# Float64 weights converted in pieces of 768 columns, with the lower parts on DVE and no arithmetic on GpSimd meanwhile

## The chip, the cores and the metric

The kernel runs as one program on one core of a Trainium2 chip. The metric is the device time of one execution in microseconds. PE is TensorE, DVE is VectorE, ACT is ScalarE, POOL is GpSimd and SP is SyncE, whose queue issues the loads.

## The reference

Three blocks follow one another. The gated layer's three weight matrices reach the kernel as float64, in pairs of 32-bit words; all else is float32.

```python
# sliding-window attention: B, H, S, D = 4, 8, 576, 64, window 64
scores = where(0 <= i - j < 64, q @ k.T / 8, -1e9)
x = softmax(scores) @ v                       # -> 2304 tokens x 512
# gated layer: w_gate, w_val 512 x 1536, w_out 1536 x 512
x = (sigmoid(x @ w_gate) * (x @ w_val)) @ w_out
# 8 experts, top 1: w1 512 x 1024, w2 1024 x 512 each
e = argmax(x @ w_gate2);  y = relu(x @ w1[e]) @ w2[e]
out = softmax(x @ w_gate2)[e] * sigmoid(x @ w_output_gate)[e] * y
```

## The kernel before

Attention is cut into 36 blocks of 64 queries, each with four pairs of heads. A block has four stages: `st_s` makes scores on PE, row maxima on DVE and exponentials with their sums on ACT; `st_n` takes the reciprocal of the sums on DVE and multiplies the probabilities by it (line 217), for the first `PM_B` = 12 blocks on POOL, for the rest on DVE; `st_t` transposes on PE and copies on ACT; `st_v` multiplies with the values and splits the result into an upper part `xh` (ACT) and a lower part `xl` (DVE). Four blocks make a chunk of 256 tokens; there are nine chunks c.

The gated layer walks over steps (c, f), f being one of 12 slices of 128 hidden columns. `g1(c, f)` runs 24 matmuls (line 300), three for each product, since every operand is split into an upper and a lower part. Then come a tanh on ACT (303), a product on DVE (304), the upper part `gh` on ACT (307) and the lower part `gl` on POOL (308). `g2` adds the slice to the chunk's sums with six matmuls (319), one step later. The steps of chunks 0 and 1 are interleaved, because the weights are still being converted; there are 24 of these, and chunks 2 to 8 follow with weights that stay in SBUF.

A slice f has 1536 float64 columns per partition: gate, value and output weights of 512 each. They are loaded and converted in 36 pieces of 512. `load_w` loads a piece of 512 KB into one of `B_STG` = 3 staging buffers; pieces 3 to 8 (`RAWS` = 2 slices) go to memory of weight tiles that are filled only later. `conv_a` takes the absolute value of the upper words on ACT (273) into one of `B_Z` = 4 buffers z. `conv_b` runs four instructions on DVE, two with one tensor input (281, 282) and two with two (283, 284), which put the float32 together; ACT copies it rounded as the upper part (286), and POOL subtracts that from z for the lower part (287). A staging buffer is free when line 284 is done, and then SP issues the next load into it.

Order: `FIRST` is the order of the first loads on SP (q: keys and queries of a block, v: values, w: a piece of weights, m and c: tables). `conv` is called after each step and keeps the converted pieces two slices ahead of the steps (`CVX` = 6 pieces); before the first step it does one piece for each of six rounds (`CV_S`). `AHEAD` = 1 says how many pieces `conv_a` is ahead of `conv_b`. The order in which instructions enter each engine's queue comes from a planner that simulates their times when the program is built; each engine then takes its queue in order.

Of the kernel before, what the change touches and what calls it, by code (L numbers as in the profile page):

```python
# [10 lines left out]
F32 = mybir.dt.float32  # L11
F32R = mybir.dt.float32r
BF16 = mybir.dt.bfloat16
I32 = mybir.dt.int32
U32 = mybir.dt.uint32
ACTF = mybir.ActivationFunctionType
ALU = mybir.AluOpType
# [8 lines left out]
P = 128  # L26
# [5 lines left out]
HP = H // 2  # L32
KD = DM // P
NF1 = F1 // P
LAST = NCH - 1, NF1 - 1
# [6 lines left out]
C2L = 0, 1, 2, 3  # L42
A0D = A1D = 2

CVX, CV_S, AHEAD = 6, 1, 1
B_STG, B_Z = 3, 4


PM_B, EARLY, RAWS = 12, 8, 2

FIRST = "q0 m w0 q1 c q2 v0 w1 q3 v1 v2 w2 v3 q4 w3 q5 w4 v4 q6 w5 v5 q7 w6 v6 v7 w7 w8"
WARM_A = 8
WARM_T = 4, 6, 20

# [37 lines left out]
def kern(ctx, tc, ins, out):  # L92
    nc = tc.nc
# [3 lines left out]
    wp = ctx.enter_context(tc.tile_pool(name="wp", bufs=1))  # L97
# [7 lines left out]
    def w_tile(f, n):  # L105

        if (f, n) not in W:
            W[f, n] = wp.tile([P, 6, 512], F32R if n else F32, tag=f"w{f}", name=f"w{f}")
        return W[f, n]
# [13 lines left out]
    stg = cvx.enter_context(tc.tile_pool(name="stg", bufs=B_STG, side="right"))  # L123
    tmp = cvx.enter_context(tc.tile_pool(name="tmp", bufs=B_Z, side="right"))
# [87 lines left out]
    def st_n(b):  # L212
        sp, sm = att[b]
        rs = smp.tile([P, HP], F32, tag="rs", name="rs")
        nc.vector.tensor_scalar(out=rs, in0=sm, scalar1=1e-9, scalar2=None, op0=ALU.add)
        nc.vector.reciprocal(out=rs, in_=rs)
        (nc.gpsimd if b < PM_B else nc.vector).tensor_tensor(out=sp, in0=sp, in1=rs.rearrange("p (h o) -> p h o", o=1).to_broadcast([P, HP, P]), op=ALU.mult)

    def st_t(b):
        sp, sm = att[b]  # L220
# [25 lines left out]
    wst, raws = {}, {}  # L246
    loaded = [0]

    def staged(n):

        return not B_STG <= n < B_STG + 3 * RAWS

    def load_w(_):
        n = loaded[0]
        if n >= 3 * NF1:
            return
        loaded[0] += 1
        if staged(n):
            t = stg.tile([P, 512, 2], I32, tag="stg", name="stg")
        else:  # L260
            f, i = divmod(n - B_STG, 3)
            if i == 0:
                raws[f] = wp.tile([P, 3, 512, 2], I32, tag=f"w{5 - f}", name=f"raw{f}")
            t = raws[f][:, i]
        nc.sync.dma_start(out=t, in_=w1_d[:, n].bitcast(I32).rearrange("p (n t) -> p n t", t=2))
        wst[n] = t

    def conv_a(n):
        if n >= 3 * NF1:
            return  # L270
        raw = wst[n]
        z = tmp.tile([P, 512], F32, tag="z", name="z")
        nc.scalar.activation(out=z, in_=raw[:, :, 1].bitcast(F32), func=ACTF.Abs)
        wst[n] = (raw, z)

    def conv_b(n):
        f, j = divmod(n, 3)
        raw, z = wst.pop(n)
        lo, hi = raw[:, :, 0], raw[:, :, 1]
        zi, hif = z.bitcast(I32), hi.bitcast(F32)  # L280
        nc.vector.tensor_scalar(out=z, in0=z, scalar1=F64_LEAST, scalar2=F64_MOST, op0=ALU.max, op1=ALU.min)  # L281
        nc.vector.tensor_scalar(out=zi, in0=zi, scalar1=3, scalar2=0x3FFFFFF8, op0=ALU.logical_shift_left, op1=ALU.bitwise_and)  # L282
        nc.vector.scalar_tensor_tensor(out=zi, in0=hi, scalar=-0x40000000, in1=zi, op0=ALU.bitwise_and, op1=ALU.bitwise_or)  # L283
        nc.vector.scalar_tensor_tensor(out=zi, in0=lo, scalar=29, in1=zi, op0=ALU.logical_shift_right, op1=ALU.bitwise_or)  # L284
        w = w_tile(f, 1)
        nc.scalar.activation(out=w[:, j], in_=z, func=ACTF.Copy)  # L286
        nc.gpsimd.tensor_tensor(out=w[:, j + 3], in0=z, in1=w[:, j].bitcast(F32), op=ALU.subtract)  # L287
        if staged(n):
            load_w(n)

    gt = {}

    def g1(c, f):
        xh, xl = xt[c]
        g1p = ps.tile([P, 2, CHT], F32, tag="g1", name="g1", bufs=2)
        for j in range(2):
            n = 0
            for k in range(KD):
                for ws, xs in ((j, xh), (j, xl), (j + 3, xh)):
                    nc.tensor.matmul(out=g1p[:, j], lhsT=W[f, 1][:, ws, k * P:(k + 1) * P], rhs=xs[:, k], start=(n == 0), stop=(n == 3 * KD - 1))  # L300
                    n += 1
        g = gp.tile([P, CHT], F32, tag="g", name="g")
        nc.scalar.activation(out=g, in_=g1p[:, 0], func=ACTF.Tanh, scale=0.5)  # L303
        nc.vector.scalar_tensor_tensor(out=g, in0=g, scalar=1.0, in1=g1p[:, 1], op0=ALU.add, op1=ALU.mult)  # L304
        gh = gp.tile([P, CHT], F32R, tag="gh", name="gh")
        gl = gp.tile([P, CHT], F32R, tag="gl", name="gl")
        nc.scalar.activation(out=gh, in_=g, func=ACTF.Copy)  # L307
        (nc.vector if (c, f) == LAST else nc.gpsimd).tensor_tensor(out=gl, in0=g, in1=gh.bitcast(F32), op=ALU.subtract)  # L308
        gt[c, f] = (gh, gl)

    acc = {}
# [307 lines left out]
    def open_stage():  # L619
        sp2 = ctx.enter_context(tc.tile_pool(name="sp2", bufs=1, side="right"))  # L620
        raw2.extend(sp2.tile([P, 1024], F32, name=f"raw{i}") for i in range(3))
        for i in range(3):
            load2(0, i)
# [297 lines left out]
    steps, n1 = [], 0  # L921
# [27 lines left out]
    for c in range(NCH - 1):  # L949
        n = at[c, NF1 - 1] + 1 if c else at[0, NF1 - 1] + 1  # L950
# [7 lines left out]
    nc.vector.memset(hot, 0.0)  # L958
    warm(ps.tile([P, 512], F32, tag="pv", name="idle"), hot, hot[:, 0:P], WARM_A)
    does = dict(q=load_kq, v=load_v, w=load_w, m=lambda _: nc.sync.dma_start(out=msk, in_=m_d[:, 0:M_MID]), c=lambda _: nc.sync.dma_start(out=cst, in_=c_d))  # L960
    for x in FIRST.split():
        does[x[0]](int(x[1:] or 0))
    cw = [0]

    def conv(n):
        n = min(n, 3 * NF1)
        while cw[0] < n:
            conv_a(cw[0] + AHEAD)
            conv_b(cw[0])
            cw[0] += 1  # L970

    for n in range(AHEAD):
        conv_a(n)
    prev = None
    for n in range(min(todo), len(steps)):
        acts = sorted(todo.get(n, []), key=lambda x: (x[0] in ROUTE, x[1]))
        for k, b in acts:
            if k == "n":
                st_n(b)
        if n >= 0:  # L980
            c, f = steps[n]
            g1(c, f)
        for k, b in acts:
            if k in ROUTE:
                ROUTE[k](b)
            elif k != "n":
                dict(s=st_s, t=st_t, v=st_v)[k](b)
        if prev is not None:
            g2(*prev)
            if prev[1] == NF1 - 1:  # L990
                if not R:
                    cvx.close()
                    open_route()
                r_row(prev[0])
        if n < 0:
            conv(cw[0] + CV_S)
        else:
            prev = (c, f)
            if c <= 1:
                conv(3 * sum(x[0] == 0 for x in steps[:n + 1]) + CVX)  # L1000
        if n == at[NCH - 1, 0]:
            atx.close()
            open_stage()
        if (c, f) >= (NCH - 1, 6) and f < NF1 - 1:
            for g in (2 * (f - 6), 2 * (f - 6) + 1):
                if g < NF2:
                    split2(0, g)
# [4 lines left out]
def layout(q, k, v, moe_w_gate, moe_w_val, moe_w_out, moe2_w_gate, moe2_w_output_gate, moe2_w1, moe2_w2):  # L1012
    flat = lambda a: a.transpose(0, 2, 1, 3).reshape(NT, HP, 2 * D)
    kf, vf, qf = flat(k), flat(v), flat(q)
    win = np.arange(P)[None] + BLK * (np.arange(NBLK)[:, None] - 1)
    win[0, :BLK] = np.arange(BLK)
    for b in range(EARLY, NBLK, KR):
        win[b] = np.roll(win[b], BLK)
    kT = kf.reshape(NBLK, BLK, HP, P).transpose(0, 3, 2, 1)
    vw = vf[win].reshape(NBLK, P, DM)  # L1020
    qT = qf.reshape(NBLK, BLK, HP, P).transpose(0, 3, 2, 1)
    kp = lambda w: w.reshape(KD, P, NF1, P).transpose(1, 2, 0, 3).reshape(P, NF1, 512)
    w1 = np.stack([kp(moe_w_gate), kp(moe_w_val), moe_w_out.reshape(NF1, P, DM).transpose(1, 0, 2)], axis=2)
    w1 = np.ascontiguousarray(w1).view(np.int64).reshape(P, 3 * NF1, 512)
    wr = np.concatenate([moe2_w_gate, moe2_w_output_gate], axis=1).reshape(KD, P, 2 * E).transpose(1, 0, 2)
    a = moe2_w1.reshape(E, KD, P, NF2, P).transpose(0, 2, 3, 1, 4).reshape(E, P, NF2, KD * P)
    b = moe2_w2.reshape(E, NF2, P, DM).transpose(0, 2, 1, 3)
    w2 = np.concatenate([a, b], axis=3)
    c, m = const_tables()
    return dict(k=kT, v=vw, q=qT, w1=w1, wr=wr, w2=w2, c=c, m=m)  # L1030
# [19 lines left out]
```

## Time and profile before

| | |
|---|---|
| median of three runs | 919.5 us (914.69, 924.28, 919.5) |
| profiled execution, own time | 917.5 us |
| its span | 915.7 us |
| mean granted clock of PE | 0.98 |
| busy share of the span: PE / DVE / ACT / POOL | 93 / 53 / 40 / 25% |

The span is the time that the trace covers; the execution's own time is 1.8 us longer. Times in the rows below count from the span's start. The shares are averages over very different stages: the first 150 us (attention and conversion), the gated layer up to some 620 us, and the experts.

### The profile page before, as it was taken

The page shows a single profiled execution, that of the slowest core. Times are in us where ns is not written, and L with a number is a line of the kernel's source. Part 1 is how long each engine was busy: PE and PEld are TensorE (multiplying, and loading weights), DVE is VectorE, ACT ScalarE, POOL GpSimd, SP SyncE. Part 2 cuts the span into 40 slices and gives each one's busy share as a digit, 9 for nine tenths or more (in the row PEclk, how much of TensorE's full clock was granted, in tenths as well). Part 3 has the DMA queues.
Part 4 walks back from the last instruction along what each step waited for, and adds up shares of the span by engine and source line. Part 5 has one row for each costly group of instructions (what it writes and reads, how often), then busy time and mean ns, then how long its engine had stood idle before and what let it go on. Part 6 is the DMA issues. An engine that isn't in the chain of part 4 may idle for free.

```text
span 915.7 us, 16106 instructions
## 1 busy us (share of the span) xinstructions
PE 849.4 (93%) x6336; PEld 784.9 (86%) x6336; DVE 483.6 (53%) x1060; ACT 368.7 (40%) x889; POOL 230.3 (25%) x239
## 2 busy tenths in 40 slices
PE   6788778999999999999999999997999999999992
PEld 4677667989999999999999999985989999989991
DVE  6999995234444335344443352624556766467620
ACT  5755443343243233332432433422345654355510
POOL 3556565201111111111111111123023333133011
PEclk8989999999999999999999999998999999999997
DMA  8935551221121111111111102503457665466201
GB/s 234 302 104 150 148 145 47 66 63 35 36 58 38 53 28 46 48 47 35 55 33 31 52 1 92 181 5 114 123 138 233 195 189 163 153 192 196 81 24 35
DMA packets 52887, 90.96 MB, mean 99 GB/s; under 512 B 24751, under 2 KB 29871, under 8 KB 52786
## 3 DMA queue, kind: packets, MB, share of 16 engines
q1 hardware_dynamic: 47666, 76.45, 29.0%
q0 software_dynamic: 5120, 13.12, 4.3%
q8 instruction: 69, 1.13, 0.5%
q14 instruction: 32, 0.26, 0.1%
HBM read 80.10 MB, written 13.11 MB: 102 GB/s over the span
## 4 chain that ended last, share of the span: by engine, by line
PE 79%; DVE 13%; issue 3%; DMA 2%; ACT 1%; POOL 1%; SPq 1%; PEldq 0%; POOLq 0%; DVEq 0%; ACTq 0%
PE g L300 28%; PE acc L319 14%; PE hps L703 12%; PE yps L716 11%; DVE z L283 3%; DVE z L281 3%; PE s L193 3%; DVE z L284 2%; PE tps L684 2%; PE pv L238 2%; DVE z L282 2%; PE yps L726 1%; PE pt L223 1%; PE x2ps L394 1%; DMA raw<-in_w_dram 1%
## 5 line engine op out<-in xcount | busy, mean ns | idle before, releaser
L300 PE MATMUL g<-xh,w 128*128 128x256 f32 x1728 | 336.3, 285 | 16.3 <-DVE g L304 14.5
L300 PEld LDWEIGHTS g<-xh,w 128*128 128x128 f32 x1728 | 278.7, 191 | 24.7 <-DVE g L304 16.6
L300 PE MATMUL g<-xl,w 128*128 128x256 f32 x864 | 245.3, 284 | 0.0
L308 POOL TENSOR_TENSOR gl<-g,gh 128x256 fp32r<-128x256 f32 x107 | 84.7, 791 | 392.6 <-ACT gh L307 380.6
L300 PEld LDWEIGHTS g<-xl,w 128*128 128x128 f32 x864 | 165.4, 192 | 4.9 <-DVE xl L242 0.2
L304 DVE SCALAR_TENSOR_TENSOR g<-g,g 128x256 f32<-128x256 f32 x108 | 45.1, 418 | 171.7 <-ACT g L303 171.3
L303 ACT ACTIVATE g<-g 128x256 f32<-128x256 f32 x108 | 41.3, 383 | 229.8 <-PE g L300 226.8
L319 PE MATMUL acc<-w,gh 128*128 128x512 f32 x432 | 125.8, 412 | 3.9 <-ACT gh L307 3.8
L703 PE MATMUL hps<-xg,w 128*128 128x256 f32 (+5 forms) x768 | 119.8, 307 | 7.9 <-issue 4.8
L703 PEld LDWEIGHTS hps<-xg,w 128*128 128x128 f32 x768 | 112.8, 192 | 11.2 <-issue 5.1
L716 PE MATMUL yps<-w,w 128*128 128x256 f32 (+5 forms) x672 | 112.1, 315 | 0.0
L716 PEld LDWEIGHTS yps<-w,w 128*128 128x128 f32 x672 | 99.4, 189 | 3.0
L797 DVE SCALAR_TENSOR_TENSOR w<-hps,w 128x512 fp32r<-128x512 f32 x64 | 44.2, 691 | 92.5 <-ACT w L796 92.5
L796 ACT ACTIVATE w<-hps 128x512 fp32r<-128x512 f32 x64 | 38.3, 598 | 121.9 <-PE hps L703 121.9
L319 PEld LDWEIGHTS acc<-w,gh 128*128 128x128 f32 x432 | 73.7, 190 | 15.9 <-ACT gh L307 5.7
L769 DVE TENSOR_TENSOR w<-raw,w 128x1024 fp32r<-128x1024 f32 x56 | 68.6, 1225 | 15.3 <-ACT w L768 15.3
L319 PE MATMUL acc<-w,gl 128*128 128x512 f32 x216 | 68.1, 396 | 0.7 <-POOL gl L308 0.6
L814 POOL DMA_INDIRECT out_dram<-ysb,gi x32 | 39.4, 1231 | 93.8 <-DVE ysb L776 44.7
L287 POOL TENSOR_TENSOR w<-z,w 128x512 fp32r<-128x512 f32 x36 | 53.2, 1478 | 38.6 <-ACT w L286 38.3
L818 POOL DMA_INDIRECT grow<-x2d,gi x32 | 33.1, 1035 | 116.9 <-PE tps L684 101.3
L768 ACT ACTIVATE w<-raw 128x1024 fp32r<-128x1024 f32 x56 | 58.9, 1051 | 0.0
L307 ACT ACTIVATE gh<-g 128x256 fp32r<-128x256 f32 x108 | 45.0, 416 | 26.7 <-DVE g L304 26.5
(172 smaller groups left out, 994.7 us busy)
## 6 DMA issues: line engine op xcount, KB each, us to landing
raw<-in_w_dram SPq DMA_DIRECT2D x70, 512.0 KB, 4.2
stg<-in_w_dram SPq DMA_DIRECT2D x30, 512.0 KB, 3.7
v<-in_v_dram SPq DMA_DIRECT2D x28, 256.0 KB, 2.8
x2d<-row SPq DMA_DIRECT2D x18, 256.0 KB, 2.5
kring<-in_k_dram SPq DMA_DIRECT2D x29, 128.0 KB, 2.6
qbd<-in_q_dram SPq DMA_DIRECT2D x56, 64.0 KB, 2.4
w<-in_v_dram SPq DMA_DIRECT2D x8, 256.0 KB, 5.5
w<-in_k_dram SPq DMA_DIRECT2D x8, 128.0 KB, 5.0
```

The lines of the kernel that those rows point to most:

```text
L287: nc.gpsimd.tensor_tensor(out=w[:, j + 3], in0=z, in1=w[:, j].bitcast(F32), op=ALU.subtract)
L300: nc.tensor.matmul(out=g1p[:, j], lhsT=W[f, 1][:, ws, k * P:(k + 1) * P], rhs=xs[:, k], start=(n == 0), stop=(n == 3 * KD - 1))
L303: nc.scalar.activation(out=g, in_=g1p[:, 0], func=ACTF.Tanh, scale=0.5)
L304: nc.vector.scalar_tensor_tensor(out=g, in0=g, scalar=1.0, in1=g1p[:, 1], op0=ALU.add, op1=ALU.mult)
L307: nc.scalar.activation(out=gh, in_=g, func=ACTF.Copy)
L308: (nc.vector if (c, f) == LAST else nc.gpsimd).tensor_tensor(out=gl, in0=g, in1=gh.bitcast(F32), op=ALU.subtract)
L319: nc.tensor.matmul(out=acc[c][i], lhsT=gs[:, i * P:(i + 1) * P], rhs=W[f, 1][:, ws], start=(f == 0 and n == 0), stop=(f == NF1 - 1 and n = ...
L703: ins = nc.tensor.matmul(out=hp[:, 0:n], lhsT=wv[:, 0, k * P:(k + 1) * P], rhs=xv[:, k, 0:n], start=(m == 0), stop=(m == len(mm) - 1))
L716: ins = nc.tensor.matmul(out=yps[d][:, 0:n], lhsT=wv[:, d * P:(d + 1) * P], rhs=hv[:, 0:n], start=(f == 0 and m == 0), stop=(f == NF2 - 1 ...
L768: a = (("Y", e - 2, KD - 1), ("ld", i)), lambda: nc.scalar.activation(out=hi, in_=r2, func=ACTF.Copy), ("sh", e, f), "act", 1
L769: v = (("ld", i), ("sh", e, f)), lambda: nc.vector.tensor_tensor(out=lo, in0=r2, in1=hi.bitcast(F32), op=ALU.subtract), ("sl", e, f), "dve", 1
L797: v.append(((("H", e, f), ("r", e, f)), lambda hh=hh, hl=hl, hp=hp: nc.vector.scalar_tensor_tensor(out=hl, in0=hp, scalar=0.0, in1=hh.bitc ...
```

## The change

Each slice is converted in two pieces of 768 columns instead of three of 512, so there are 24 pieces of 768 KB. There are two staging buffers and two z of that size (before: three and four of 512), and the slices loaded straight into weight tiles are pieces 2 to 5. `conv` does a slice at a time: the four DVE instructions of both pieces, then for each piece the subtraction of the lower part, now on DVE, and behind it the absolute value of the piece two further on. The lower part `gl` of chunks 0 and 1 is subtracted on DVE. The probabilities of the first 12 blocks are scaled by four ACT instructions, one for each pair of heads. `FIRST` lists six pieces of weights instead of nine, the same bytes, in another place among the loads of attention. Before the first step two rounds convert a slice each.

```diff
--- before.py
+++ after.py
@@ -42,13 +42,17 @@
 C2L = 0, 1, 2, 3
 A0D = A1D = 2
 
-CVX, CV_S, AHEAD = 6, 1, 1
-B_STG, B_Z = 3, 4
+CVX, AHEAD = 4, 2
+
+CV_S = 2, 0, 0, 2, 0, 0
+B_STG, B_Z = 2, 2
 
 
 PM_B, EARLY, RAWS = 12, 8, 2
 
-FIRST = "q0 m w0 q1 c q2 v0 w1 q3 v1 v2 w2 v3 q4 w3 q5 w4 v4 q6 w5 v5 q7 w6 v6 v7 w7 w8"
+UN, NU = 768, 2
+
+FIRST = "q0 m w0 q1 c q2 v0 w1 q3 v1 v2 w2 v3 q4 w3 q5 v4 q6 w4 v5 q7 w5 v6 v7"
 WARM_A = 8
 WARM_T = 4, 6, 20
 
@@ -214,7 +218,11 @@
         rs = smp.tile([P, HP], F32, tag="rs", name="rs")
         nc.vector.tensor_scalar(out=rs, in0=sm, scalar1=1e-9, scalar2=None, op0=ALU.add)
         nc.vector.reciprocal(out=rs, in_=rs)
-        (nc.gpsimd if b < PM_B else nc.vector).tensor_tensor(out=sp, in0=sp, in1=rs.rearrange("p (h o) -> p h o", o=1).to_broadcast([P, HP, P]), op=ALU.mult)
+        if b < PM_B:
+            for h in range(HP):
+                nc.scalar.activation(out=sp[:, h], in_=sp[:, h], func=ACTF.Copy, scale=rs[:, h:h + 1])
+        else:
+            nc.vector.tensor_tensor(out=sp, in0=sp, in1=rs.rearrange("p (h o) -> p h o", o=1).to_broadcast([P, HP, P]), op=ALU.mult)
 
     def st_t(b):
         sp, sm = att[b]
@@ -248,45 +256,46 @@
 
     def staged(n):
 
-        return not B_STG <= n < B_STG + 3 * RAWS
+        return not B_STG <= n < B_STG + NU * RAWS
 
     def load_w(_):
         n = loaded[0]
-        if n >= 3 * NF1:
+        if n >= NU * NF1:
             return
         loaded[0] += 1
         if staged(n):
-            t = stg.tile([P, 512, 2], I32, tag="stg", name="stg")
+            t = stg.tile([P, UN, 2], I32, tag="stg", name="stg")
         else:
-            f, i = divmod(n - B_STG, 3)
+            f, i = divmod(n - B_STG, NU)
             if i == 0:
-                raws[f] = wp.tile([P, 3, 512, 2], I32, tag=f"w{5 - f}", name=f"raw{f}")
+                raws[f] = wp.tile([P, NU, UN, 2], I32, tag=f"w{5 - f}", name=f"raw{f}")
             t = raws[f][:, i]
         nc.sync.dma_start(out=t, in_=w1_d[:, n].bitcast(I32).rearrange("p (n t) -> p n t", t=2))
         wst[n] = t
 
     def conv_a(n):
-        if n >= 3 * NF1:
+        if n >= NU * NF1:
             return
         raw = wst[n]
-        z = tmp.tile([P, 512], F32, tag="z", name="z")
+        z = tmp.tile([P, UN], F32, tag="z", name="z")
         nc.scalar.activation(out=z, in_=raw[:, :, 1].bitcast(F32), func=ACTF.Abs)
         wst[n] = (raw, z)
 
     def conv_b(n):
-        f, j = divmod(n, 3)
         raw, z = wst.pop(n)
         lo, hi = raw[:, :, 0], raw[:, :, 1]
-        zi, hif = z.bitcast(I32), hi.bitcast(F32)
+        zi = z.bitcast(I32)
+        w = w_tile(n // NU, 1).rearrange("p s n -> p (s n)")
+        a = n % NU * UN
+        wh, wl = w[:, a:a + UN], w[:, NU * UN + a:NU * UN + a + UN]
         nc.vector.tensor_scalar(out=z, in0=z, scalar1=F64_LEAST, scalar2=F64_MOST, op0=ALU.max, op1=ALU.min)
         nc.vector.tensor_scalar(out=zi, in0=zi, scalar1=3, scalar2=0x3FFFFFF8, op0=ALU.logical_shift_left, op1=ALU.bitwise_and)
         nc.vector.scalar_tensor_tensor(out=zi, in0=hi, scalar=-0x40000000, in1=zi, op0=ALU.bitwise_and, op1=ALU.bitwise_or)
         nc.vector.scalar_tensor_tensor(out=zi, in0=lo, scalar=29, in1=zi, op0=ALU.logical_shift_right, op1=ALU.bitwise_or)
-        w = w_tile(f, 1)
-        nc.scalar.activation(out=w[:, j], in_=z, func=ACTF.Copy)
-        nc.gpsimd.tensor_tensor(out=w[:, j + 3], in0=z, in1=w[:, j].bitcast(F32), op=ALU.subtract)
+        nc.scalar.activation(out=wh, in_=z, func=ACTF.Copy)
         if staged(n):
             load_w(n)
+        return lambda: nc.vector.tensor_tensor(out=wl, in0=z, in1=wh.bitcast(F32), op=ALU.subtract)
 
     gt = {}
 
@@ -305,7 +314,7 @@
         gh = gp.tile([P, CHT], F32R, tag="gh", name="gh")
         gl = gp.tile([P, CHT], F32R, tag="gl", name="gl")
         nc.scalar.activation(out=gh, in_=g, func=ACTF.Copy)
-        (nc.vector if (c, f) == LAST else nc.gpsimd).tensor_tensor(out=gl, in0=g, in1=gh.bitcast(F32), op=ALU.subtract)
+        (nc.vector if (c, f) == LAST or c <= 1 else nc.gpsimd).tensor_tensor(out=gl, in0=g, in1=gh.bitcast(F32), op=ALU.subtract)
         gt[c, f] = (gh, gl)
 
     acc = {}
@@ -963,11 +972,13 @@
     cw = [0]
 
     def conv(n):
-        n = min(n, 3 * NF1)
+        n = min(n, NU * NF1)
         while cw[0] < n:
-            conv_a(cw[0] + AHEAD)
-            conv_b(cw[0])
-            cw[0] += 1
+
+            for i, low in enumerate([conv_b(cw[0] + i) for i in range(NU)]):
+                low()
+                conv_a(cw[0] + AHEAD + i)
+            cw[0] += NU
 
     for n in range(AHEAD):
         conv_a(n)
@@ -993,11 +1004,11 @@
                     open_route()
                 r_row(prev[0])
         if n < 0:
-            conv(cw[0] + CV_S)
+            conv(cw[0] + CV_S[n])
         else:
             prev = (c, f)
             if c <= 1:
-                conv(3 * sum(x[0] == 0 for x in steps[:n + 1]) + CVX)
+                conv(NU * sum(x[0] == 0 for x in steps[:n + 1]) + CVX)
         if n == at[NCH - 1, 0]:
             atx.close()
             open_stage()
@@ -1021,7 +1032,7 @@
     qT = qf.reshape(NBLK, BLK, HP, P).transpose(0, 3, 2, 1)
     kp = lambda w: w.reshape(KD, P, NF1, P).transpose(1, 2, 0, 3).reshape(P, NF1, 512)
     w1 = np.stack([kp(moe_w_gate), kp(moe_w_val), moe_w_out.reshape(NF1, P, DM).transpose(1, 0, 2)], axis=2)
-    w1 = np.ascontiguousarray(w1).view(np.int64).reshape(P, 3 * NF1, 512)
+    w1 = np.ascontiguousarray(w1).view(np.int64).reshape(P, NU * NF1, UN)
     wr = np.concatenate([moe2_w_gate, moe2_w_output_gate], axis=1).reshape(KD, P, 2 * E).transpose(1, 0, 2)
     a = moe2_w1.reshape(E, KD, P, NF2, P).transpose(0, 2, 3, 1, 4).reshape(E, P, NF2, KD * P)
     b = moe2_w2.reshape(E, NF2, P, DM).transpose(0, 2, 1, 3)
```

## Rows read from the trace of the kernel before

**Rows 1.** Busy time by stretch: length, PE, weight loads, DVE, ACT, POOL; clock, DMA.

```profile
46.00:98.00 52.00, 43.33 (x295) 38.20 (x294) 51.59 (x77) 26.08 (x63) 30.82 (x24) 0.94 0.44 129
98.00:149.30 51.30, 39.19 (x262) 34.32 (x262) 50.62 (x69) 23.02 (x51) 30.71 (x23) 1.00 0.45 132
```

**Rows 2.** Chain of waits, 46 to 149.3 us, its shares by line.

```profile
by line: DVE z L283 26.8%; DVE z L281 22.3%; DVE z L284 16.7%; issue 12.9%; DVE z L282 11.0%; DVE g L304 3.2%; DVE rs L215 2.4%; DVE nm L198 1.8%; DVE nm L199 1.8%; DVE xl L242 0.8%; ACT z L273 0.7%; ACT w L286 0.6%; DVE rs L216 0.3%
```

**Rows 3.** DVE groups, 46 to 149.3 us: busy, mean ns; idle before.

```profile
L284 DVE SCALAR_TENSOR_TENSOR z<-stg,z 128x512 int32<-128x512 int32 x27 | 26.6, 983 | 0.2
L283 DVE SCALAR_TENSOR_TENSOR z<-stg,z 128x512 int32<-128x512 int32 x27 | 25.5, 944 | 0.7
L281 DVE TENSOR_SCALAR z<-z 128x512 f32<-128x512 f32 x28 | 25.0, 893 | 0.1
L282 DVE TENSOR_SCALAR z<-z 128x512 int32<-128x512 int32 x28 | 15.8, 563 | 0.1
```

**Rows 4.** DVE instruction by instruction, 87 to 92 us: start, duration.

```profile
87.03 0.41 DVE L304 SCALAR_TENSOR_TENSOR g<-g,g 128x256 f32<-128x256 f32 x1
87.36 0.68 DVE L284 SCALAR_TENSOR_TENSOR z<-stg,z 128x512 int32<-128x512 int32 x1
87.96 0.41 DVE L282 TENSOR_SCALAR z<-z 128x512 int32<-128x512 int32 x1
88.41 1.12 DVE L283 SCALAR_TENSOR_TENSOR z<-stg,z 128x512 int32<-128x512 int32 x1
...
91.16 0.41 DVE L281 TENSOR_SCALAR z<-z 128x512 f32<-128x512 f32 x1
91.49 0.41 DVE L304 SCALAR_TENSOR_TENSOR g<-g,g 128x256 f32<-128x256 f32 x1
```

**Rows 5.** POOL in the same stretch.

```profile
88.03 0.95 POOL L308 TENSOR_TENSOR gl<-g,gh 128x256 fp32r<-128x256 f32 x1 [1.21 <-ACT gh L307]
```

**Rows 6.** POOL groups, 46 to 149.3 us.

```profile
L287 POOL TENSOR_TENSOR w<-z,w 128x512 fp32r<-128x512 f32 x28 | 41.7, 1489 | 32.8 <-ACT w L286 32.4
L308 POOL TENSOR_TENSOR gl<-g,gh 128x256 fp32r<-128x256 f32 x16 | 17.1, 1069 | 7.1 <-ACT gh L307 4.8 <-DMA kring<-in_k_dram 2.3
```

**Rows 7.** Who waited for whom, 46 to 149.3 us: total, times, longest.

```profile
PE g L300 <- DVE g L304: 14.5, 10, 2.6
...
ACT z L273 <- DMA stg<-in_w_dram: 10.3, 9, 2.2
```

**Rows 8.** DVE groups after 150 us.

```profile
L769 DVE TENSOR_TENSOR w<-raw,w 128x1024 fp32r<-128x1024 f32 x56 | 68.6, 1225 | 15.3 <-ACT w L768 15.3
...
L215 DVE TENSOR_SCALAR rs<-sm 128x4 f32<-128x4 f32 x25 | 4.3, 170 | 42.0 <-ACT sp L207 42.0
```

**Rows 9.** Chain of waits, 250 to 262 us: start, length, what.

```profile
250.09 2.87 PE g L300 x24
...
253.86 1.39 PE acc L319 x6
```

**Rows 10.** DMA issues: line, count, size, median us to landing.

```profile
stg<-in_w_dram SPq DMA_DIRECT2D x30, 512.0 KB, 3.7
v<-in_v_dram SPq DMA_DIRECT2D x28, 256.0 KB, 2.8
```

**Rows 11.** Loads of the staging tile.

```profile
DMA to landing us min/median/max: 3.4/3.7/8.8
```

**Rows 12.** ACT groups, 46 to 149.3 us.

```profile
L286 ACT ACTIVATE w<-z 128x512 fp32r<-128x512 f32 x28 | 17.6, 629 | 30.4 <-DVE z L284 30.4
...
L307 ACT ACTIVATE gh<-g 128x256 fp32r<-128x256 f32 x15 | 6.2, 412 | 8.3 <-DVE g L304 8.1
```

**Rows 13.** Busy time by stretch, 8 to 46 us.

```profile
8.00:46.00 38.00, 28.07 (x244) 23.23 (x242) 34.22 (x68) 26.65 (x96) 19.30 (x16) 0.90 0.96 289
```

**Rows 14.** ACT instruction by instruction: two of a block's four exponentials.

```profile
40.85 0.37 ACT L207 ACTIVATE w<-s,nm 128x128 f32<-128x128 f32 x1 [2.67 <-DVE nm L199]
...
41.21 0.36 ACT L207 ACTIVATE w<-s,nm 128x128 f32<-128x128 f32 x1
```

## The prediction

> **What bounds the kernel now.** I read the busy times by stretch first. From 46 to 149.3 us DVE is busy 51.59 of 52.00 and 50.62 of 51.30 us, PE 43.33 and 39.19 [rows 1]. The chain of waits through that stretch runs over the four conversion instructions of DVE, lines 281 to 284, with 77% between them [rows 2]. So the reader is to see one stage of 103.3 us that DVE sets, ahead of a long rest that PE sets; a microsecond won on DVE here is won at the end, as long as PE or something else isn't late next. PE shows the other side: it waits 14.5 us for line 304, which stands in DVE's queue among the conversions [rows 7].
>
> Then I asked why DVE takes so long. The groups give means of 983, 944, 893 and 563 ns for the four instructions [rows 3]. One by one they are much shorter where POOL rests: 0.68 us for line 284, 0.41 for 281 and 282 [rows 4]. Line 283 has the same two inputs and length as 284, but took 1.12 us at 88.41, while POOL subtracted from 88.03 to 88.98 [rows 4, 5]: it got through about 0.55 us after POOL had ended. POOL works 62 us in the stage [rows 1], 41.7 in the lower parts of the weights and 17.1 in `gl` [rows 6]. With 28 pieces at bare durations (2 x 0.68 + 2 x 0.41 = 2.18 us) DVE would need 61 us for conversion where its four groups took 93 and some more in pieces from other buffers: some 32 us or more are DVE held while POOL works.
>
> **Prices on DVE without POOL.** What counts is the distance from one start to the next. Two inputs, 512 columns: 0.60 us (87.36 to 87.96). One input: 0.33 (91.16 to 91.49), or 0.45 when the next one needs the result (87.96 to 88.41). Line 304, 256 columns: 0.33 (87.03 to 87.36) [rows 4]. For 256 columns more, the two-input price comes from line 769: (1.225 - 0.68) / 2 = 0.27; the one-input price from line 215, nearly without columns: (0.41 - 0.17) / 2 = 0.12 [rows 4, 8]. So with 768 columns a two-input instruction takes 0.87, a one-input one 0.45, or 0.57 in front of its reader. The four of a piece take 0.45 + 0.57 + 2 x 0.87 = 2.76 us; if each waits for the one before (0.12 more each, as between the two one-input prices), 3.1 to 3.2. The subtraction that comes from POOL has two inputs: 0.87.
>
> **The stage on DVE.** The stage has 28 pieces of 512 [rows 3], thus 18.67 of 768, or 9.33 slices. Conversion: 18.67 x (2.76 + 0.87) = 67.8 us. 16 steps [rows 6], each with one line 304 and now one `gl` of the same size: 32 x 0.33 = 10.6. Three blocks of attention, each with one reduction of 512 columns, one `xl` of 256 and three tiny ones: 3 x (0.68 + 0.41 + 3 x 0.17) = 4.8. Sum 83.2 us, 20.1 less than 103.3. If nothing in a piece overlaps, 18.67 x 0.4 = 7.5 more: 90.7. So the change puts some 21.5 us of subtraction on DVE and takes the holding off, which is worth more.
>
> **What is late next.** PE: 16 steps of 2.87 + 1.39 us [rows 9] are 68 us, with the attention of three blocks somewhat over 70. That is below 83, so PE doesn't bound it, though it limits any gain to some 30 us.
>
> The loads do come close. Before there were three staging buffers; now a buffer goes round once for each slice: load, absolute value, four DVE instructions, and only then the next load. The load of 512 KB takes 3.7 us, one of 256 KB 2.8 [rows 10]; 768 KB are 4.6 by that slope and 5.6 in proportion to size. The absolute value: ACT takes 629 ns for 512 columns and 412 for 256 [rows 12], so 0.85. DVE 2.76 to 3.2. No row shows the three hand-overs by themselves; I take 0.3 in all, between 0 and 0.6. The round is 8.5 to 10 us a slice. Now it is 103.3 / 9.33 = 11.07 us, and DVE alone would need 83.2 / 9.33 = 8.9. Two loops of nearly the same length, tied by queues that are taken in order, don't overlap wholly: the subtraction of the second piece waits for ACT's copy of 0.85, covered by the subtraction of the first (0.87), and the next absolute value stands behind both; with two z instead of four nothing runs further ahead. If that cover is gone, as when a tanh stands before the copy, DVE and the next product 304 wait up to half a microsecond a piece. I take 9.6 us a slice, in the upper half of the round. 9.33 x 9.6 = 89.6 us, a gain of 13.7.
>
> The Trainium skill (DMA: Bandwidth & Descriptors, Anatomy of one DMA) gives a GpSimd-issued transfer 2.0 us plus its bytes at 436 GB/s, so by estimate 3.8 us for 768 KB. By it 512 KB would take 3.2 where the row has 3.7, on another queue, and the round would fall to 7.8 us, under DVE's 8.9; that is the first rival.
>
> **The front, 0 to 46 us.** Moving the scaling to ACT costs 4 instructions for each of eight blocks. Exponentials of the same shape start 0.36 us apart, with their sum's read-out between [rows 14]: at most 8 x 4 x 0.36 = 11.5 us. ACT is busy 26.65 of 38.00 us there [rows 13], so it becomes full, and the transposes wait for it as they now wait for POOL. DVE is relieved there too, of some of POOL's 19.30 us. But the DMA engines are 0.96 busy at 289 GB/s [rows 13], and the bytes are the same. In the new order the keys and queries of block 4 come 768 KB later, 2.7 us at that rate. I bound the front from 4 us gained to 5 lost and take nothing. Fewer issues on SP (24 instead of 36) are nothing either, since it waits for buffers. Four late blocks also go to ACT, which is busy 49 of 103 us in the stage [rows 1]. After the stage nothing differs but six or so `gl` on DVE, which is no longer full.
>
> **The sum.** The profiled execution took 917.5 us with a span of 915.7; 917.5 - 13.7 = 903.8. The median of the three runs is 2 us above it, with a spread of 5 on either side, so I don't correct: 904 us.
>
> **Rivals.** (1) Loads and ACT hide altogether, and DVE's bare sum sets the stage: a gain of 20.1, 897 us. For it: the DMA engines are under half busy in the stage [rows 1]. Against it: two buffers and in-order queues. 20%. The Trainium skill's formula, above, speaks for it too.
>
> (2) ACT's queue becomes the wait: the absolute value stands behind the freed buffer by little more than one piece, so ACT stops at loads, with tanh and `gh` of the running step behind it. That wait exists already, nine times and up to 2.2 us [rows 7]. One more microsecond a slice than I took, 10.6: 98.9 us, a gain of 4.4, 913 us. 15%.
>
> (3) Slower: the loads land late. One load in the trace took 8.8 us [rows 11]. If 768 KB took that through the stage, the round would be 8.8 + 0.85 + 2.8 + 0.3 = 12.8 us; over the eight slices that reuse staging buffers 8 x (12.8 - 11.07) = 13.8 us more, 931 us. It decides from a landing time of 7.1 us on. Against it: the stage's DMA share is 0.44 and 0.45 [rows 1], where the front's is 0.96. 6%.
>
> (4) The change doesn't do what it says: DVE was held by something else than POOL. Then its extra 18.67 x 0.87 + 16 x 0.33 = 21.5 us come on top: 939 us. Rows 4 and 5 speak against it. 4%.
>
> My forecast has the other 55%, with its own range of 9.0 to 10.3 us a slice (gains of 19.3 to 7.2) and the front's bounds.
>
> **How the numbers follow.** The range takes in rival 1 with some gain in the front, and rival 2: 894 to 914; outside lie rivals 3 and 4 and little else. A measurement of this kernel can tell about 1%, 9 us, from no change. Faster by over that: rival 1, most of the forecast and a little of rival 2: 0.70. Within: 0.21. Slower: 0.09.
>
> **What would show it.** In the profile after: POOL without arithmetic until conversion ends; the two-input instructions of 768 columns at 0.95 us with hardly any spread, the one-input ones at 0.53; conversion ending some 14 us earlier, at 135; a slice every 9.6 us. DVE no longer full: some 90% busy, its idle time ended by ACT's absolute values, and those by loads, which land in 4.6 to 5.6 us. If DVE stays full, rival 1 is right; if its instructions stay stretched, rival 4. The prediction is wrong if the front grows by more than 5 us because ACT is full there, or if the planner's order leaves DVE waiting for a whole load in each slice.

## The result, and the profile after

The changed kernel takes 894.8 us (median of four, 891.55 to 896.97) against 921.45 beside it: a ratio of 0.973, 95% interval 0.970 to 0.976. Run again on another chip it was 896.9 us, 0.978 (0.975 to 0.981). The profiled execution took 894.2 us with a span of 892.4, 23.3 us less span than before. The sign is right, and the time lies in the range of 894 to 914, though only just inside its lower end. The gain is 23 us between the two profiled executions (27 and 21 by the medians beside each other), where the sum had 13.7.

The same two stretches as [rows 1], in the changed kernel:

```profile
46.00:98.00 52.00, 50.95 (x405) 47.23 (x401) 47.81 (x87) 32.16 (x79) 0.00 (x0) 1.00 0.56 173
98.00:149.30 51.30, 49.70 (x358) 45.76 (x357) 39.20 (x70) 25.59 (x55) 0.97 (x7) 1.00 0.34 110
```

POOL is silent until conversion is over (its seven instructions are fills for the next stage). PE, 43 and 39 us busy before, has 2.7 us of idle time left in the two stretches together, where it had 20.8. DVE is no longer full: 47.8 of 52, and then it runs out of conversion.

The DVE groups that answer to [rows 3], from 46 us to the end of conversion (line 298 is the lower part that came from POOL; 293 and 294 are the old 283 and 284, 291 and 292 the old 281 and 282):

```profile
L298 DVE TENSOR_TENSOR w<-z,w 128x768 fp32r<-128x768 f32 x18 | 17.1, 953 | 0.5 <-ACT w L295 0.4
L293 DVE SCALAR_TENSOR_TENSOR z<-stg,z 128x768 int32<-128x768 int32 x18 | 17.1, 951 | 0.1
L294 DVE SCALAR_TENSOR_TENSOR z<-stg,z 128x768 int32<-128x768 int32 x18 | 17.1, 950 | 0.0
L292 DVE TENSOR_SCALAR z<-z 128x768 int32<-128x768 int32 x18 | 10.0, 554 | 0.2
L291 DVE TENSOR_SCALAR z<-z 128x768 f32<-128x768 f32 x17 | 9.5, 559 | 5.5 <-ACT z L281 5.2
```

The chain of waits, 46 to 130 us, its shares by line [rows 2]:

```profile
by line: DMA stg<-in_w_dram 36.0%; ACT z L281 10.7%; DVE z L293 7.5%; PE g L309 7.2%; DVE z L294 6.4%; DVE w L298 6.0%; issue 5.2%; DVE z L291 4.7%; DVE z L292 3.5%; PE acc L328 3.3%; DVE g L313 2.6%; ACT sp L211 1.8%; ACT w L295 1.8%; DVE 
```

Before, four lines of DVE had 77% of the chain. Now loads have 36%, ACT's absolute value 11, five conversion lines of DVE 28, and PE 10. That is one round: load, absolute value, DVE, next load. DVE over one slice shows it (start, duration):

```profile
95.04 0.56 DVE L291 TENSOR_SCALAR z<-z 128x768 f32<-128x768 f32 x1 [0.95 <-ACT z L281]
...
96.32 0.95 DVE L298 TENSOR_TENSOR w<-z,w 128x768 fp32r<-128x768 f32 x1
97.19 0.95 DVE L293 SCALAR_TENSOR_TENSOR z<-stg,z 128x768 int32<-128x768 int32 x1
98.06 0.41 DVE L313 SCALAR_TENSOR_TENSOR g<-g,g 128x256 f32<-128x256 f32 x1
98.39 0.95 DVE L294 SCALAR_TENSOR_TENSOR z<-stg,z 128x768 int32<-128x768 int32 x1
99.42 0.56 DVE L291 TENSOR_SCALAR z<-z 128x768 f32<-128x768 f32 x1
...
104.67 0.56 DVE L291 TENSOR_SCALAR z<-z 128x768 f32<-128x768 f32 x1 [0.61 <-ACT z L281]
```

The first pieces of two successive slices start at 95.04 and 104.67, 9.6 us apart, and before each DVE has idled until ACT was done. Who waited for whom, 46 to 149.3 us (total, times, longest), and the staging loads (count, size, median to landing, then least, median, most):

```profile
ACT z L281 <- DMA stg<-in_w_dram: 16.7, 10, 3.1
...
DVE z L291 <- ACT z L281: 5.2, 9, 1.0
...
PE g L309 <- DVE g L313: 2.7, 4, 1.1
```

```profile
stg<-in_w_dram SPq DMA_DIRECT2D x20, 768.0 KB, 4.3
```

```profile
DMA to landing us min/median/max: 4.1/4.3/8.9
```

PE's waits for the product went from 14.5 us [rows 7] to 2.7; ACT now waits 16.7 us for loads.

Two marks measure the stage. The last lower part, on POOL before and on DVE after:

```profile
150.07 1.28 POOL L287 TENSOR_TENSOR w<-z,w 128x512 fp32r<-128x512 f32 x1 [1.29 <-ACT w L286]
```

```profile
133.22 0.96 DVE L298 TENSOR_TENSOR w<-z,w 128x768 fp32r<-128x768 f32 x1 [0.25 <-ACT w L295]
```

So conversion ends at 151.35 and 134.18 us. And the first and the last of the 24 tanh of chunks 0 and 1, before:

```profile
42.24 0.40 ACT L303 ACTIVATE g<-g 128x256 f32<-128x256 f32 x1
...
179.78 0.39 ACT L303 ACTIVATE g<-g 128x256 f32<-128x256 f32 x1 [1.79 <-PE g L300]
```

and after:

```profile
47.54 0.53 ACT L312 ACTIVATE g<-g 128x256 f32<-128x256 f32 x1
...
156.04 0.39 ACT L312 ACTIVATE g<-g 128x256 f32<-128x256 f32 x1 [0.81 <-PE g L309]
```

The last one comes 23.7 us earlier, which is the whole of the gain within half a microsecond. The first one comes 5.3 us later. The front, to be held against [rows 13]:

```profile
8.00:46.00 38.00, 28.07 (x223) 22.09 (x223) 32.50 (x69) 35.84 (x127) 0.00 (x0) 0.82 0.95 291
```

ACT went from 26.65 to 35.84 of 38 us.

Both traces up to the last tanh, before and after (columns as in [rows 1]):

```profile
0.00:180.20 180.20, 145.25 (x1038) 126.21 (x1038) 146.54 (x237) 87.93 (x240) 91.69 (x87) 0.96 0.51 151
```

```profile
0.00:156.40 156.40, 140.53 (x1053) 124.39 (x1054) 124.62 (x236) 96.91 (x264) 3.54 (x16) 0.96 0.57 174
```

Of these 23.8 us, 19.1 are idle time of PE that went away (34.95 to 15.87). The other 4.7 are a shorter busy time for nearly the same number of matmuls. In the kernel before the granted clock of PE was 1.2 GHz from 45.3 to 48.7 and from 59.0 to 62.4 us; in the changed one it was 2.4 GHz throughout the stage (1.00 in both rows above). How much of the 4.7 us that explains, no run shows.

### The profile page after: what moved, and what is told of

The parts are those of the page before. It is cut to its first block, busy times and chain, and to the rows that moved or that the text cites. A ratio compares the mean times of both kernels' runs of the same rounds, so it can differ in the third digit from the quotient of the medians.

```text
span 892.4 us, 15979 instructions
## 1 busy us (share of the span) xinstructions
PE 843.6 (95%) x6336; PEld 782.3 (88%) x6336; DVE 461.6 (52%) x1060; ACT 377.6 (42%) x913; POOL 141.3 (16%) x167
## 4 chain that ended last, share of the span: by engine, by line
PE 81%; ACT 5%; DVE 5%; DMA 5%; issue 2%; POOL 1%; PEldq 0%; SPq 0%; POOLq 0%; ACTq 0%; DVEq 0%
PE g L309 30%; PE acc L328 15%; PE hps L712 13%; PE yps L725 11%; DMA stg<-in_w_dram 4%; PE s L197 3%; PE tps L693 2%; PE pv L246 2%; PE yps L735 2%; ACT z L281 1%; PE pt L231 1%; ACT w L211 1%; PE x2ps L403 1%; ACT w L223 1%; DVE z L293 1%
## 5 line engine op out<-in xcount | busy, mean ns | idle before, releaser
L309 PE MATMUL g<-xh,w 128*128 128x256 f32 x1728 | 332.6, 284 | 3.7 <-DVE g L313 2.7
L313 DVE SCALAR_TENSOR_TENSOR g<-g,g 128x256 f32<-128x256 f32 x108 | 45.1, 419 | 163.8 <-ACT g L312 163.4
L317 POOL TENSOR_TENSOR gl<-g,gh 128x256 fp32r<-128x256 f32 x83 | 61.6, 742 | 388.7 <-ACT gh L316 379.0
L328 PEld LDWEIGHTS acc<-w,gh 128*128 128x128 f32 x432 | 73.4, 189 | 10.3 <-ACT gh L316 0.5
L211 ACT ACTIVATE sp<-sp,nm 128x128 f32<-128x128 f32 x96 | 37.4, 391 | 28.0 <-DVE nm L207 28.0
```

The costliest lines, as they stand in the source:

```text
L211: nc.scalar.activation(out=sp[:, h], in_=src[:, h], func=ACTF.Exp, bias=nm[:, h:h + 1], scale=scale, accum_out=sm[:, h:h + 1])
L317: (nc.vector if (c, f) == LAST or c <= 1 else nc.gpsimd).tensor_tensor(out=gl, in0=g, in1=gh.bitcast(F32), op=ALU.subtract)
L328: nc.tensor.matmul(out=acc[c][i], lhsT=gs[:, i * P:(i + 1) * P], rhs=W[f, 1][:, ws], start=(f == 0 and n == 0), stop=(f == NF1 - 1 and n = ...
```

## The experiments

Eleven runs. In the table: ratio to the kernel before beside it on the same chip, with its interval, since the kernel before itself had medians from 917.5 to 921.5 us; then the median, the first tanh, the end of the last lower part, and the last of the 24 tanh, from each run's trace.

| run | ratio | us | first tanh | lower parts end | 24th tanh |
|---|---|---|---|---|---|
| before | 1 | | 42.2 | 151.4 | 179.8 |
| changed | 0.973 (0.970 to 0.976) | 894.8 | 47.5 | 134.2 | 156.0 |
| c1_after_again | 0.978 (0.975 to 0.981) | 896.9 | 47.3 | 133.6 | 155.5 |
| e1_quiet_512 | 0.976 (0.974 to 0.979) | 895.7 | 44.8 | 141.3 | 159.7 |
| e2_768_pool | 0.989 (0.986 to 0.993) | 909.1 | 41.2 | 147.9 | 170.3 |
| e3_pool_idle_sub | 0.987 (0.982 to 0.992) | 906.3 | 48.0 | 142.4 | 164.2 |
| e6_gl_pool | 0.981 (0.977 to 0.984) | 898.7 | 46.8 | 135.7 | 157.5 |
| e4_scale_pool | 0.976 (0.974 to 0.978) | 895.6 | 38.2 | 138.6 | 160.4 |
| e5_scale_dve | 0.983 (0.980 to 0.986) | 902.4 | 38.5 | 143.5 | 165.3 |
| e8_low_twice | 0.994 (0.991 to 0.996) | 912.7 | 46.1 | 153.5 | 173.8 |
| c2_small_attn | 0.978 (0.976 to 0.981) | 897.8 | 49.2 | 136.0 | 158.3 |
| e7_stg3 | 0.975 (0.973 to 0.977) | 895.5 | 47.6 | 129.9 | 155.9 |
| e9_stg3_scale_pool | 0.971 (0.969 to 0.973) | 892.0 | 37.5 | 130.1 | 151.7 |

The marks come from one execution of each run. From the 24th tanh to the end these executions take 734.6 to 740.3 us, so a shift of a mark and one of the time can differ by some 5 us.

**POOL silent, pieces of 512.** The old kernel with only the moves of work:

```diff
-        nc.gpsimd.tensor_tensor(out=w[:, j + 3], in0=z, ...)
+        nc.vector.tensor_tensor(out=w[:, j + 3], in0=z, ...)
-        (nc.vector if (c, f) == LAST else nc.gpsimd).tensor_tensor(out=gl, ...)
+        (nc.vector if (c, f) == LAST or c <= 1 else nc.gpsimd).tensor_tensor(out=gl, ...)
+            (scaling of blocks under PM_B: four ACT instructions, as in the change)
```

> Before, with POOL's subtractions moved as in the change (lower parts of the weights and gl of chunks 0 and 1 to DVE, scaling of 12 blocks to ACT), but pieces of 512 columns, three staging buffers, four z and the old order of loads. Theory (the gain is DVE no longer held by POOL): line 283 and 284 at 0.69 us without spread, conversion ends at 131 to 138 us instead of 151, time 890 to 900, a gain of 21 to 31. Rival (the larger pieces give most of it, by fewer instructions and loads): the gain stays under 12, time above 909.

0.976, between the two measurements of the change. The two-input instruction has no spread, as expected (durations: least, median, most, ns; line 287 is the old 283):

```profile
L287 DVE SCALAR_TENSOR_TENSOR z<-stg,z x30: 684/690/701, 9.5 to 138.2; 128x512 int32<-128x512 int32 x30
```

So with POOL silent the size of the pieces adds nothing that can be told here, although with 512 conversion ends 7 us later (141.3, and not by 138 as expected). That was a first sign that the end of conversion alone doesn't set the time: in this run's DVE queue 19 products stand ahead of the last conversion, and the last tanh follows the end by only 18.4 us.

**Pieces of 768, work on POOL.** The reverse:

```diff
-        return lambda: nc.vector.tensor_tensor(out=wl, ...)
+        return lambda: nc.gpsimd.tensor_tensor(out=wl, ...)
         (gl and scaling back on POOL as before)
```

> The change without its second half: pieces of 768, two staging buffers and two z, but lower parts, gl and scaling on POOL. Theory (DVE is held as long as POOL subtracts): the two-input instructions of 768 columns spread from 0.95 to over 2 us, conversion ends within 5 us of before's 151. In DVE's queue 18 products (the line of g) stand ahead of the last conversion where before has 16, so even then two steps of 4.3 us less lie behind it: time 910 to 921. Rival (size alone gains): conversion ends before 142 and the time is under 906.

0.989 and 909 us, just under the range given; the rival's 906 isn't reached. Conversion ends at 147.9, 3.5 us before the old 151.35, but the last tanh comes 22.4 us behind that instead of 28.4. The two-input instruction behind POOL's work (durations: least, median, most, ns):

```profile
L289 DVE SCALAR_TENSOR_TENSOR z<-stg,z x20: 944/2479/2522, 9.7 to 141.4; 128x768 int32<-128x768 int32 x20
```

0.95 us by itself, 2.5 in the median. So the larger pieces, with the new order that comes with them, gain 1.1% even while POOL works; that and the 2.4% of the run before don't add up in the change.

**POOL subtracting for nobody.**

```diff
         nc.scalar.activation(out=wh, in_=z, func=ACTF.Copy)
+        nc.gpsimd.tensor_tensor(out=idle, in0=wh[:, 0:512].bitcast(F32), in1=wh[:, 0:512].bitcast(F32), op=ALU.subtract)
```

> The change, plus one subtraction of 512 columns on POOL for each of the 24 pieces, as soon as ACT has the upper part; its result goes to memory that nobody reads, and no instruction waits for it. The order of DVE's queue is that of the changed kernel. Theory (DVE is held whenever POOL subtracts): 24 x 1.3 to 1.5 us of POOL hold DVE for about half of that, 13 to 20 us, of which some 7 us of idle time in the stage absorb a part; the two-input instructions reach 1.5 to 2 us, time 6 to 15 us above the changed kernel. Rival (what stretched DVE was the waiting for POOL's results, not POOL's work beside it): the time stays within 3 us of the changed kernel and the durations have no spread.

906 us, 9 to 12 above the two medians of the changed kernel, in the range of the theory; the rival is out. POOL at 84 us and DVE beside it:

```profile
84.45 1.11 POOL L297 TENSOR_TENSOR poolidle<-w 128x512 f32<-128x512 f32 x1 [3.71 <-ACT w L296]
```

```profile
84.57 1.80 DVE L300 TENSOR_TENSOR w<-z,w 128x768 fp32r<-128x768 f32 x1
86.29 0.95 DVE L294 SCALAR_TENSOR_TENSOR z<-stg,z 128x768 int32<-128x768 int32 x1
```

POOL works from 84.45 to 85.56. The subtraction on DVE, started at 84.57, lasts 1.80 us and ends 0.81 after POOL; it is the wait for POOL's whole instruction and then nearly all of the usual 0.95. Nothing waits for POOL's result here, so it is the work beside it that holds DVE. Adding up what DVE's instructions last beyond their bare durations up to the end of conversion, 23 of them are lengthened, by 19 us together, for 32 us of POOL's work. Conversion ends 8.2 us later, and the last tanh too.

**Half of it: `gl` on POOL.**

```diff
-        (nc.vector if (c, f) == LAST or c <= 1 else nc.gpsimd).tensor_tensor(out=gl, ...)
+        (nc.vector if (c, f) == LAST else nc.gpsimd).tensor_tensor(out=gl, ...)
```

> The change with gl of chunks 0 and 1 back on POOL, all else as changed. DVE is relieved of 22 x 0.33 = 7 us and held by 22 subtractions of 256 columns of 0.75 to 1.1 us. Theory (hold about half of POOL's time, 10 us): between 1 us faster and 7 us slower than the changed kernel, 894 to 902. Rival (a little work on POOL is free since DVE has gaps): 4 to 8 us faster, 887 to 891.

0.981, 898.7 us: in the theory's range, and the rival's gain isn't there. These 24 short subtractions on POOL cost about as much as they relieve: 19 of them start before conversion ends and take 19 x 0.33 = 6.3 us off DVE, and by the trace DVE is held for 5.8 us until then.

**The change once more**, for the chip of the next three:

> The changed kernel itself once more, beside the next three on one chip. Both theories: 0.973 of before, the span near 892, first tanh at 47.5, conversion's end at 134.

As expected but for the ratio, 0.978, and the span, 895.0; the marks moved by no more than 0.6 us.

**Scaling back on POOL.**

```diff
-        if b < PM_B:
-            for h in range(HP):
-                nc.scalar.activation(out=sp[:, h], in_=sp[:, h], func=ACTF.Copy, scale=rs[:, h:h + 1])
+        (nc.gpsimd if b < PM_B else nc.vector).tensor_tensor(out=sp, in0=sp, in1=rs..., op=ALU.mult)
```

> The change with the scaling of the first 12 blocks back on POOL, all else as changed. In the changed kernel the first tanh comes at 47.5 us where before had 42.2, with ACT busy 35.8 of 38 us. Theory (ACT is the bound of the front, put there by the 32 scalings): first tanh at 41 to 45 us, time 1 to 6 us under the changed kernel, less what 12 subtractions' worth of POOL (13 us) hold DVE. Rival (the front is bound by the loads, which come in another order): first tanh stays above 46 and the time is the same or up to 4 us more, by the hold.

Half right. The first tanh comes at 38.2, 9 us earlier (41 to 45 had been expected), with ACT at 28.73 in the front:

```profile
8.00:46.00 38.00, 29.99 (x263) 25.05 (x261) 36.50 (x71) 28.73 (x93) 10.94 (x8) 0.91 0.94 285
```

So ACT bounded the front. But the time is the same as the change's within the noise, and in the trace conversion ends 5 us later (138.6) and the last tanh with it. That trace is of the slowest of the five executions (900.7 us, median 895.6), and in it PE's granted clock was 0.94 from 46 to 138.6 us, where the run beside it had 1.00 from 46 to 133.6: 1.2 GHz for two stretches, 2.4 GHz for the rest. So the 5 us may be this execution's and not the edit's.

**Scaling on DVE.**

```diff
+        nc.vector.tensor_tensor(out=sp, in0=sp, in1=rs..., op=ALU.mult)   # all blocks
```

> The change with the scaling of the first 12 blocks on DVE, one instruction of 0.69 us each, so that POOL stays silent and ACT gets its 4 x 0.3 us a block back. Theory (ACT bounds the front): first tanh at 42 to 46 us; DVE in the front goes from 32.5 to some 37.5 of 38 us and is nearly full; time 1 to 5 us under the changed kernel. Rival (loads bound the front): first tanh above 46, time 0 to 3 us more, by 12 x 0.6 us on DVE.

The first tanh again early, 38.5; the time rises to 0.983, 5.5 us over the run beside it. Both sides miss: the theory's gain is not there, the rival had at most 3 us more, and the early tanh speaks against its reason. Conversion ends at 143.5. Why that is 5 us later than with the scaling on POOL I can't say: the edit reorders the queues, and ACT's waits for loads between 46 and 151 us rise to 32.7, from 21.2 in the run beside it.

**Lower parts twice.**

```diff
+            for _ in range(2):
                 nc.vector.tensor_tensor(out=wl, in0=z, in1=wh.bitcast(F32), op=ALU.subtract)
```

> The change with each subtraction of the lower part done twice on DVE: 24 x 0.87 = 21 us more there, some 16 of them in the stage from 46 to 134 us, where DVE has 7 us of idle time. Theory (PE sets the stage and conversion only has to stay ahead of the steps): conversion ends 7 to 12 us later, but the time rises by no more than 4 to 9 us. Rival (conversion's end sets the time, as the prediction had it): the time rises by as much as conversion's end moves, 8 to 14 us.

My theory of that moment fell; the rival is right in kind, though both had the shifts too small. 21 us more on DVE move conversion's end by 19.9 us against the run beside it, the last tanh by 18.3 and the time by 15.8. DVE's idle time absorbed nothing to speak of: it is 6.6 us in the stage (46 to 153.5) against 6.8 in the run beside it. That fits a round in which DVE is one part, the more so as the second subtraction also keeps z, of which there are two; no run separates these. Nor is it a rule: in e3 the hold took DVE's idle time in the stage down to 1.2 us.

**A third staging buffer**, with a control for the room that it needs:

```diff
-    vp = ... bufs=3 ...   spp = ... bufs=2
+    vp = ... bufs=2 ...   spp = ... bufs=1          # control and run
-B_STG, B_Z = 2, 2
+B_STG, B_Z = 3, 2                                   # run alone
-FIRST = "... w5 v6 v7"
+FIRST = "... w5 v6 v7 w6"
```

> A control for the next run: the change with two buffers of values instead of three and one of probabilities instead of two, which makes room for a staging buffer but doesn't use it. Both theories: conversion's end within 2 us of 134, time within 4 us of the changed kernel, 893 to 901.

> The control with a third staging buffer of 768 columns and one more load among the first. Theory (the round load, absolute value, four DVE instructions, next load sets the slice at 9.6 us): ACT's waits for loads vanish, a slice falls to DVE's own 8.7 to 9.1 us, conversion ends 4 to 8 us earlier, at 126 to 130, and the time falls by 3 to 7 us against the control. Rival (DVE or PE, both over 90% busy, set the slice): conversion's end and the time stay within 2 us of the control.

The control behaves like the change, with conversion's end 2 us later. With the third buffer ACT's waits for loads, 22.2 us in the control (46 to 135 us),

```profile
ACT z L281 <- DMA stg<-in_w_dram: 22.2, 16, 2.5
```

are down to a single one of 0.8, and ACT waits for PE and, for a free z, for the lower part:

```profile
ACT g L312 <- PE g L309: 27.3, 17, 3.0
ACT z L281 <- DVE w L298: 4.4, 6, 0.9
```

Conversion ends 6.1 us earlier, as the theory said, so the round of loads did set it. The time falls by only 2.3 us, less than the 3 to 7 expected, and the two intervals overlap. The two stretches in the control and then with the third buffer say why:

```profile
46.00:98.00 52.00, 50.86 (x411) 46.90 (x410) 46.27 (x83) 31.65 (x72) 0.00 (x0) 1.00 0.52 159
98.00:134.00 36.00, 33.64 (x235) 31.14 (x234) 33.20 (x53) 17.37 (x30) 0.00 (x0) 1.00 0.46 150
```

```profile
46.00:98.00 52.00, 52.00 (x412) 47.89 (x412) 49.73 (x89) 32.81 (x73) 0.00 (x0) 0.99 0.51 157
98.00:134.00 36.00, 36.00 (x256) 33.60 (x255) 30.93 (x53) 16.55 (x29) 0.97 (x7) 1.00 0.34 113
```

PE is now busy in every microsecond of the two stretches, and the chain of waits from 46 to 130 us holds nothing else:

```profile
by line: PE g L309 62.2%; PE acc L328 28.7%; PE pv L246 3.4%; PE s L197 3.2%; PE pt L231 2.1%; PE s L195 0.5%
```

With the front's first tanh still at 47.6, PE can't be quicker.

**Both: third buffer, scaling on POOL.**

> The third staging buffer together with the scaling of the first 12 blocks on POOL, which brought the first tanh to 38 us but ended conversion 4.4 us later. Theory (loads set the slice): with the round opened, DVE's own 8.7 to 9.1 us a slice count, conversion ends at 127 to 132, and PE's earlier start is of use: 2 to 6 us under the changed kernel. Rival (POOL's hold in the front puts conversion back, and nothing makes it up): conversion ends at 136 or later, time 0 to 4 us over the run with the third buffer alone.

892.0 us, ratio 0.971, the best of all, and the last tanh at 151.7. Conversion ends at 130.1, as early as without POOL in the front; the earlier first tanh is now of use. It lies 3.5 us below the third buffer alone, and 2.8 and 4.9 us below the change's two medians, as expected. Against the change's two measurements, 0.973 and 0.978, it is 0.2 to 0.7% better, and only the second interval is clear of it.

## Why the prediction was right, and where its size was off

**The hold was read rightly.** The two-input instructions take 951 ns with no spread to speak of (forecast 0.95), the one-input ones 554 and 559 (0.53). Runs e1, e2 and e3 show from three sides that it is POOL's work that stretched DVE: rival 4 is out. The moves by themselves give all of the gain that can be told (e1); the pieces by themselves give less than half of it (e2).

**The slice was read rightly.** From 85 us on the first pieces of the slices come 9.5 to 9.7 us apart, as forecast; over all eight slices from 45.1 to 123.8 us the mean is 9.8, within the 9.0 to 10.3 given. The reason was the one given too: a round of load, absolute value and DVE; e7 opens it and conversion ends 6 us earlier. The load takes 4.3 us, under the 4.6 to 5.6 worked out, so from 512 to 768 KB it grows by 0.6 us. It is over the 3.8 us estimated, for a transfer that GpSimd issues, from the Trainium skill (DMA: Bandwidth & Descriptors, Anatomy of one DMA). Rivals 1 to 3 did not come about: rival 1's 897 us lies nearest to the time, but its mechanism, loads that hide, would have given slices of 8.9 us. Conversion was to end at 135; it ended at 134.2.

**The step that was mis-sized** is "a microsecond won on DVE here is won at the end", taken as the shift of the last conversion from 149.3 to 135.6, 13.7 us. The runs put two terms in its place. Conversion's own shift is 17.17 us: 2.05 more because in the kernel before a last lower part on POOL followed line 284 (151.35), and 1.42 more because it ended earlier than I had it. The other term I left out: how much PE still has to do then. Before, 18 of the 24 tanh had been done by the end of conversion, and the last came 28.43 us later; after, 19, and it came 21.86 us later. That is 6.57 us more, and 17.17 + 6.57 = 23.74 is what the last tanh shows. What goes with it is the order of DVE's queue: before, 16 products 304 start ahead of the last line 284, after, 18 [rows 4 show such a product between conversions]. Since DVE takes its queue in order, that number says how far the steps can be when conversion ends. All runs in pieces of 768 have those 18. In all but e7 19 tanh are done by then, and the last follows the end of conversion by 20.3 to 22.4 us, whatever end that is; in e7, where PE is full, 18 are done and it follows by 26.0. With 16 and 19 products ahead it is 28.4 and 18.4 us (before, e1). No run changes that number alone, so that it is the cause is argued and not shown.

[Rows 1] held the number that I should have used beside it: PE's idle time, 8.7 + 12.1 = 20.8 us in the stage, 2.7 after. I worked out PE's sum for the steps that happened to lie in the stage and called it no bound; in truth a quicker stage takes in more steps, and PE came within 3 us of being full.

**That the time is inside the range was luck.** My forecast's own gains were 7.2 to 19.3 us; only with 4 us gained in the front on top would they reach 23. The lower end stood at 894 for rival 1 with such a front; neither came about, and 894.8 us lies inside by less than one microsecond.

**The front** was bounded from 4 us gained to 5 lost and set to nothing. It lost 5.3 us at the first tanh, by the cause that I named: ACT full with the scalings; e4 and e5 take it away and the tanh comes at 38. A front longer by over 5 us for that cause was one of the two signs that I had set for being wrong, and it came, if by 0.3 us. That it cost nothing at the end was luck too: as long as the round of loads sets conversion, an earlier start of PE gains no time (e4, 895.6 against 896.9). With the round open the front counts, 3.5 us in e9 against e7.

**What stays open**: why conversion slows by 5 us with an earlier PE in e4 and by 10 in e5, against c1. The order of the queues changes with each edit, and I had no run that holds the order fixed there; in e4 the lower clock of the traced execution may be part of it. Also untested is a third z beside the third staging buffer.

## What to carry to other kernels

An instruction that grows to twice its length beside another engine's work may be held and not slow: look at the other engine's interval, and price the removal by the bare duration. When a stage is shared by two engines, don't price the gain by the shift of the first one's last instruction alone (17 us here); look at the idle time of the second that can go away, here 19 of the 24 us up to the last tanh. A round through a buffer (load, use, release) has to be summed like an engine; here it came to 9.6 us beside 8.9 of DVE. Opening it with a third buffer brought conversion's end forward by 6.1 us, but the time by only 2.3, because PE was the next to be full.

## What the runs showed of the hardware

DVE waits for POOL's whole instruction, not for a share of the bandwidth. In e3, 13 two-input instructions of 768 columns went from 0.95 to between 1.63 and 1.81 us, and all of them ended 0.81 to 0.82 us after POOL's instruction. The start decides: all 23 DVE instructions that were lengthened there up to the end of conversion (by over 0.06 us), and all 60 in the kernel before, started while POOL was subtracting. The 33 conversion instructions of the kernel before in which POOL's work only began kept their length.

The Trainium skill (SBUF — State Buffer, Who interferes with whom) says the same, an exclusive lock on a shared pair of ports, and that an instruction with at most one SBUF input outside the two-port modes is spared. The trace of the kernel before agrees, in few cases. Line 304, with one input in PSUM, started once while POOL subtracted and was not held; line 282 behind it was:

```profile
78.92 1.42 POOL L287 TENSOR_TENSOR w<-z,w 128x512 fp32r<-128x512 f32 x1 [2.79 <-ACT w L286]
```

```profile
79.21 0.39 DVE L304 SCALAR_TENSOR_TENSOR g<-g,g 128x256 f32<-128x256 f32 x1
79.51 1.10 DVE L282 TENSOR_SCALAR z<-z 128x512 int32<-128x512 int32 x1
```

Line 242, which also has one input in PSUM, took its usual 0.41 us at 50.62 and 56.32 us, while POOL was subtracting. Lines 199, 281 and 282 have one input too, in SBUF, and were held; whether they ran in such a mode, no trace shows. The length matters little: line 199, on 4 columns, takes 0.16 us by itself and reached 1.18, ending 0.03 us after POOL. POOL's subtraction of 512 columns took 1.26 to 1.81 us before and 1.03 at the least in e3; but e3's reads one tile twice, so what shortens it isn't shown.
